# A searched instruction order, searched again: one more edge on a PSUM bank, other order, buffers and spins

## The chip, the cores and the metric

The kernel runs on one core of one Trainium2 chip. The metric is the device time of one execution in microseconds (us). Engines are called by the profile's letters: PE is TensorE (PEld its weight loads), DVE is VectorE, ACT is ScalarE, POOL is GpSimd, SP is SyncE, which here only starts DMA transfers.

## The reference

Two blocks follow each other. The first is a linear attention with squared sketches, over 4 batches, 4 heads, 1088 positions and head size 32 (sketch size r = 8):

```python
def phi(x):
    a = np.einsum('rd,bhsd->bhsr', S1, x)
    b = np.einsum('rd,bhsd->bhsr', S2, x)
    return np.einsum('bhsi,bhsj->bhsij', a, b).reshape(*x.shape[:-1], r * r)
q_p, k_p = (phi(q), phi(k))
kv = np.einsum('bhsf,bhsd->bhfd', k_p, v)
z = np.sum(k_p, axis=2)
num = np.einsum('bhsf,bhfd->bhsd', q_p, kv)
den = np.einsum('bhsf,bhf->bhs', q_p, z)[..., None] + 1e-06
return (num / den).astype(np.float32)
```

The second takes that output with the heads side by side (4 x 1088 x 128) as x and mixes positions by two 1088 x 1088 weights:

```python
theta = x @ w_theta
cos_t, sin_t = (np.cos(theta), np.sin(theta))
zr = x * cos_t
zi = x * sin_t
yr = np.einsum('ts,bsd->btd', w_tok_r, zr)
yi = np.einsum('ts,bsd->btd', w_tok_i, zi)
y = yr + yi
u = x + y
return (u + np.maximum(u @ w_ch, 0.0)).astype(np.float32)
```

All is in 32-bit floats; weights may come as 64-bit words, which ACT and DVE turn into floats row by row.

## The kernel before, in words

The kernel does not issue its work as its loops run. Each step is recorded by `op(engine, duration, function, writes, reads)` (class `Layout`), which notes for it the steps that it must follow, by the buffers that it writes and reads or by keys that name a part of a buffer. 1015 steps are recorded and numbered so. Then three tables, written out by hand into the file from a search that was made beforehand, decide all the rest. `ORDER` lists the steps' numbers in the order in which they are issued, for all engines in one list; each engine runs its own steps in that order, and a step that waits holds up all behind it on its engine. `PLACES` gives each buffer its home, one of the numbered slots of its class (22 of `big`, 8 PSUM banks `ps`, and so on); two buffers in one home follow each other, and the second's first step waits for the first's last one. `SPINS` lists steps ahead of which TensorE does some matmuls on zeros (line 377), "step:count". `issue` walks through `ORDER` and calls each step's function. Waits between engines come from a layer below, which looks at each tile that an instruction touches. For a PSUM bank it takes the whole bank: an instruction that reads a bank waits for the last matmul issued ahead of it into that bank, and a matmul issued behind it into that bank waits for the read.

The work, in the program's order (batches are 0 to 3):

- Loads by SP, in SP's order: keys `k_l`, queries `q_l`, values `v_l` of each batch (576 KB each), keys of batches 2 and 3 once more (`r`), the two small weights, and 17 rows of the token weights (1088 KB each, into five `zs` homes). For each row ACT makes two passes and DVE two sums (row 0 to row 16).
- `key_sums`, `kfeatures`, `chain`, `chain_out`: keys are split into a rounded part and a rest, their Gram matrix is summed on TensorE (64 or 128 columns at a time), features are made and multiplied with the values (`kv`); a chain of some 25 short steps that go to and fro between DVE, ACT and TensorE (`chain`) gives the normaliser. Chains are run for batch 0, batch 1 and batches 2 and 3 together.
- `query_scale`, `query_slices`, `levels`, the den steps: queries are scaled and turned, multiplied with the normaliser's slices, and DVE works out the denominator in nine wide steps.
- `outputs_x`: for each of three groups `num`, an outer product on DVE, is turned by TensorE (line 1042; batches 2 and 3 turn it by DMA) and multiplied with the key-value matrix; `theta`, cosine, sine give z.
- Batches 0 and 1: `mix_row` multiplies all 17 rows with z on TensorE, 384, 384 and 320 columns wide.
- Batches 2 and 3 are a pair: `balance` sets their scale, and `winograd` mixes them in Strassen's way with seven products for eight: `zsub` and `asum` make differences of z and of the weight rows on DVE, `product` does the matmuls of one product into two PSUM banks (`PARTS`: columns 0 to 288 and 288 to 544), and `add` (line 1260) adds a bank, or a piece of one, into the output on DVE. Only the last product, number 4 for batch 2, is cut once more, at column 416 (`LAST`), so that its second bank holds two pieces, 288 to 416 and 416 to 544. Each piece is added by itself and is then turned, multiplied with the channel weight and stored (`done`, `finish_turned`), the end of the program.

What the change touches: `ORDER` (line 27), `PLACES`, `SPINS` and `add`. In `add`, the list of reads names the piece's keys:

```python
op("V", dve(w) + 0.05, lambda: tt(V, u(), u(), ps()[:, o:o + w], ALU.add), k_, parts_of(ps, o, w))
```

The prediction's steps are found so: first keys at `load(0, "k")`; the first outer product at `vop(CH * R * R, lambda f=outer: f(V, 0, 1), ...)` in `outputs_x`, its transpose at line 1042; the levels of batch 1 at `lev` in `levels`; joins at `join` (a DMA from POOL that adds into its target); the stop in the tail at `add` of product 4.

Of the kernel before, what the change touches and what calls it, by code (L numbers as in the profile page):

```python
# [17 lines left out]
ALU = mybir.AluOpType  # L18
# [8 lines left out]
TINY = 2.0**-60  # L27
UP = 256.0
ORDER = (
# [37 lines left out]
)  # L67
PLACES = (
# [9 lines left out]
)  # L78
SPINS = (
    "76:2 15:2 84:2 89:6 135:1 189:1 166:3 439:2 521:1 1005:1 "  # L80
)
WARM = 0
SPLIT = ()
# [5 lines left out]
PARTS = ((0, 288), (288, 544))  # L89
# [130 lines left out]
def dve(n):  # L220
    return (n + 145) / 960.0
# [15 lines left out]
def kernel(  # L237
# [52 lines left out]
    op, buf = L.op, L.buf  # L290
# [4 lines left out]
    V, A, G, T, SY = nc.vector, nc.scalar, nc.gpsimd, nc.tensor, nc.sync  # L295

    def fixed(shape, dt, name):
        b = Buf(None, shape, dt, name)
        n = math.prod(shape) * WORD[dt]
        b.ap = view(const.tile([P, (n + 3) // 4], F32, tag=name, name=name), shape, dt)  # L300
        return b

    def tt(eng, o, a, b, f):
        eng.tensor_tensor(out=o, in0=a, in1=b, op=f)  # L304
# [5 lines left out]
    def stt(o, a, s, b, op0, op1, eng=None):  # L310
        (eng or V).scalar_tensor_tensor(out=o, in0=a, scalar=s, in1=b, op0=op0, op1=op1)  # L311
# [117 lines left out]
    def powers(mfn, m, n, name):  # L429
# [7 lines left out]
        def inv():  # L437
# [16 lines left out]
                                    op=ALU.max, apply_absolute_value=True), [m2], [(sp, 0)])  # L454
# [435 lines left out]
    even = fixed((6,), F32, "even")  # L890
# [5 lines left out]
    def cells(x, t0, t1):  # L896
        return [(x, j) for j, (e0, e1) in enumerate(zip(EDGES, EDGES[1:])) if t0 < e1 and t1 > e0]
# [305 lines left out]
    def winograd():  # L1203
# [30 lines left out]
        def parts_of(ps, o, w):  # L1234
            e = sorted({0, GW} | {x - c0 for c0, c1 in PARTS for x in LAST if c0 < x < c1})
            return [(ps, a) for a, b in zip(e, e[1:]) if o < b and o + w > a]
# [22 lines left out]

        def add(b, h, j, c0, c1, ps):  # L1260
            o, w = c0 - PARTS[j][0], c1 - c0
            c0, c1 = c0 + h * HT, c1 + h * HT
            u = lambda: xT[b]()[:, c0:c1]
            k_ = cells(xT[b], c0, c1)
            if b == p:
                op("V", dve(w) + 0.05, lambda: tt(V, u(), u(), ps()[:, o:o + w], ALU.add), k_, parts_of(ps, o, w))
            else:
                op("V", dve(w) + 0.06, lambda: stt(u(), ps()[:, o:o + w], even()[:, 5:6], u(), ALU.mult, ALU.add), k_,
                   parts_of(ps, o, w) + [even])

        def done(b, h, last=()):
            for m, (_, c0, c1) in enumerate(pieces(last)):
# [20 lines left out]
        for j in range(len(PARTS)):  # L1293
            at("accl", q, "_", j)
            ps = buf("ps", (GW,), F32, "pl")
# [99 lines left out]
```

## Time and profile before

| what | us |
| --- | --- |
| median of three runs | 221.3 (220.59, 221.3, 222.36) |
| the profiled execution, its own time | 219.88 |
| its span, first to last instruction | 218.1 |
| PE busy | 209.8 |
| DVE busy | 179.1 |
| ACT busy | 112.0 |
| POOL busy | 22.8 |

The mean granted clock of TensorE is 0.995 of full speed. The span is 1.8 us shorter than the execution's own time. In the profile a matmul of 32-bit floats shows as two records, a transpose or one of 16-bit numbers as one. A matmul's record begins when it begins, but its length is longer than the step to the next one, since matmuls are pipelined: a busy PE need not be at its peak, and steps are read from the starts. A wait is shown in brackets behind an instruction, with what released it.

### The profile page before, as it was taken

Reading aid. Unit: us, or ns where it says so; the run is one execution under the profiler, and the core shown is the slowest. Engines: PE = TensorE matmul, PEld = TensorE weight load, DVE = VectorE, ACT = ScalarE, POOL = GpSimd, SP = SyncE. Lnnn points to the kernel's source line nnn. Section 1 sums busy time; section 2 is a strip of 40 time slices with the busy share of each in tenths; the row PEclk is TensorE's granted clock in tenths of the full one; section 3 lists DMA queues with packets and bytes.
Section 4 is the critical chain, followed back from the end, with each engine's and each line's share of the span. In section 5 each row is a group of like instructions: output and inputs, shape, how many; then the busy total and the mean of one; then the engine's idle time right before and its main releaser. Section 6 shows DMA issues by size and latency. Waiting matters only on the chain.

```text
span 218.1 us, 5091 instructions
## 1 busy us (share of the span) xinstructions
PE 209.8 (96%) x2012; PEld 155.3 (71%) x2012; DVE 179.1 (82%) x404; ACT 112.0 (51%) x216; POOL 22.8 (10%) x44
## 2 busy tenths in 40 slices
PE   6999899999999999999999999999999999999993
PEld 3788687677767676665866665678767888888882
DVE  4789999999999999999399709985829999996531
ACT  3898998999988998953640032433168100000000
POOL 1552000005500000010302001000400000000000
PEclk9999999999999999999999999999999999999998
DMA  5999399895999709955423998668980000405163
GB/s 162 426 416 410 110 419 410 297 370 179 257 307 405 302 13 388 378 146 161 101 33 50 188 179 199 118 107 172 236 155 0 0 0 3 72 2 86 20 92 75
DMA packets 48108, 40.59 MB, mean 186 GB/s; under 512 B 40789, under 2 KB 42453, under 8 KB 45909
## 3 DMA queue, kind: packets, MB, share of 16 engines
q1 hardware_dynamic: 42820, 35.18, 51.3%
q0 software_dynamic: 1728, 4.65, 9.8%
q10 hardware_dynamic: 3536, 0.43, 1.3%
q8 instruction: 16, 0.26, 0.5%
q14 instruction: 8, 0.06, 0.1%
HBM read 30.43 MB, written 5.18 MB: 163 GB/s over the span
## 4 chain that ended last, share of the span: by engine, by line
PE 85%; DVE 10%; DMA 2%; issue 1%; ACT 0%; SPq 0%; ACTq 0%; DVEq 0%
PE ps L339 77%; PE ps L1042 2%; DVE big L304 2%; DMA big<-k_l 2%; DVE g L304 2%; PE ps L1076 2%; PE ps L945 1%; DVE lv L304 1%; PE ps L377 1%; PE ps L721 1%; DVE sm L311 1%; DVE big L308 1%; DVE hf L308 1%; DVE sm L304 1%; SPq L392 0%
## 5 line engine op out<-in xcount | busy, mean ns | idle before, releaser
L339 PE MATMUL ps<-big,zs 128*128 128x384 f32 (+4 forms) x398 | 111.1, 425 | 0.4 <-DVE big L304 0.4
L339 PEld LDWEIGHTS ps<-big,zs 128*128 128x128 f32 x398 | 71.2, 190 | 29.9 <-issue 2.6
L1179 ACT COPY g<-ps 128x128 f32<-128x128 f32 (+1 forms) x3 | 0.9, 301 | 43.8 <-DMA out<-g 39.5
L584 ACT ACTIVATE big<-zs 128x1088 int32<-128x1088 uint32 (+1 forms) x18 | 21.1, 1187 | 3.4 <-DVE g L304 2.2
L304 DVE CUSTOM_DVE_ANT_0 big<-big,big 128x2176 uint16<-128x2176 uint16 x17 | 21.7, 1284 | 0.1
L582 ACT ACTIVATE big<-zs 128x1088 f32<-128x1088 f32 x17 | 20.7, 1223 | 0.6 <-DVE big L304 0.6
L339 PE MATMUL ps<-big,big 128*64 128x64 f32 (+2 forms) x208 | 20.9, 275 | 0.0
L339 PEld LDWEIGHTS ps<-big,big 128*64 128x64 f32 (+1 forms) x208 | 16.7, 154 | 2.8 <-issue 0.4
L304 DVE TENSOR_TENSOR big<-big,big 128x544 f32<-128x544 f32 x24 | 16.6, 709 | 1.2 <-PE ps L339 1.1
L980 ACT COPY lv<-ps 128x480 f32<-128x480 f32 x12 | 6.6, 565 | 16.1 <-PE ps L339 16.1
L318 POOL DMA_DIRECT2D big<-hf x6 | 5.7, 994 | 80.1 <-issue 37.3
L308 DVE TENSOR_SCALAR big<-big 128x1088 int32<-128x1088 int32 x17 | 12.2, 730 | 0.0
L339 PEld LDWEIGHTS ps<-w,big 128*128 128x128 f32 x80 | 10.8, 192 | 1.2
L339 PE MATMUL ps<-w,big 128*128 128x128 f32 x80 | 11.5, 277 | 0.0
L304 DVE TENSOR_TENSOR g<-lv 128x768 f32<-128x768 f32 x12 | 11.3, 947 | 0.1
L1089 ACT ACTIVATE g<-ps 128x384 f32<-128x384 f32 x12 | 5.9, 494 | 9.6 <-PE ps L339 4.4
L311 DVE SCALAR_TENSOR_TENSOR g<-g,ps 128x384 f32<-128x384 f32 x12 | 6.6, 547 | 4.7 <-ACT g L1089 4.7
L339 PE MATMUL ps<-g,sm 128*64 128x384 f32 x48 | 10.0, 502 | 0.0
L377 PE MATMUL ps<-idle 128*128 128x384 bf16 x32 | 8.7, 387 | 1.3 <-POOL idle L379 1.3
L318 POOL DMA_DIRECT2D g<-big x6 | 5.2, 923 | 44.8 <-ACT g L1157 26.8
L339 PEld LDWEIGHTS <-hf 128*64 128x64 f16 (+1 forms) x288 | 7.4, 110 | 3.2 <-issue 1.9
L304 DVE TENSOR_TENSOR zs<-ps,g 128x768 f32<-128x768 f32 (+2 forms) x15 | 9.4, 627 | 0.0
(188 smaller groups left out, 338.5 us busy)
## 6 DMA issues: line engine op xcount, KB each, us to landing
zs<-w_tok SPq DMA_DIRECT2D x17, 1088.0 KB, 7.6
big<-k_l SPq DMA_DIRECT2D x6, 576.0 KB, 8.9
big<-hf POOLq DMA_DIRECT2D x6, 576.0 KB, 5.4
big<-q_l SPq DMA_DIRECT2D x4, 576.0 KB, 7.0
big<-v_l SPq DMA_DIRECT2D x4, 576.0 KB, 5.4
fq<-g SPq DMA_DIRECT2D x24, 96.0 KB, 2.9
g<-fq SPq DMA_DIRECT2D x6, 384.0 KB, 3.8
g<-big POOLq DMA_DIRECT2D x4, 192.0 KB, 4.9
```

Source lines behind the costliest of these rows:

```text
L304: eng.tensor_tensor(out=o, in0=a, in1=b, op=f)
L308: (eng or V).tensor_scalar(out=o, in0=a, scalar1=s1, scalar2=s2, op0=op0, **kw)
L311: (eng or V).scalar_tensor_tensor(out=o, in0=a, scalar=s, in1=b, op0=op0, op1=op1)
L318: op("G", 0.9, lambda: G.dma_start(dst(), src(), accum_op=ALU.add), w, r, fly=fly)
L339: T.matmul(o, lhs, rhs, start=start, stop=stop, skip_group_check=True)
L377: T.matmul(nowhere() if home is None else view(home, (GW,), F32), idle()[:, 0:P], idle(), start=True, stop=True, skip_group_check=True)
L582: op("A", 0.22 + n * 0.0009, lambda: A.activation(dfn(), words_of(raw(), n)[1].bitcast(F32), AF.Prelu, scale=2.0**-112, alpha=-(2.0**32)), ...
L584: op("A", 0.22 + n * 0.0009, lambda: A.activation(stp(), words_of(raw(), n)[0].bitcast(U32), AF.Copy, scale=2.0**-29), [stp], [raw])
L980: op("A", act(480), lambda g=g, lp=lp: A.copy(lv().rearrange("p l (c n) -> p l c n", n=HR)[:, :, g * GC:(g + 1) * GC], lp().rearrange("p c ...
L1042: T.transpose(tr()[:, i * P:(i + 1) * P], qp()[:, i * H + 2 * n:i * H + 2 * n + 2].rearrange("p h i j -> p (h i j)"), ident())
L1076: T.transpose(x()[:, i * P:(i + 1) * P], xs()[:, off + i * P:off + (i + 1) * P], ident())
L1089: op("A", act(GW), lambda cs=cs, th=th: A.activation(cs()[:, 0], th(), AF.Copy, bias=ROUND), [(cs, 0)], [th])
```

## The change

One line is added in `add`, and its result is used in both branches: a sum whose columns end where its bank's columns end reads the whole bank, not only its piece. For the banks with one piece nothing becomes different by that. For product 4's second bank it means that the sum of columns 416 to 544 must stand behind the last matmul of columns 288 to 416 in any order that the search may give.

```diff
         def add(b, h, j, c0, c1, ps):
             o, w = c0 - PARTS[j][0], c1 - c0
+            r = [ps] if c1 == PARTS[j][1] else parts_of(ps, o, w)
             c0, c1 = c0 + h * HT, c1 + h * HT
             u = lambda: xT[b]()[:, c0:c1]
             k_ = cells(xT[b], c0, c1)
             if b == p:
-                op("V", dve(w) + 0.05, lambda: tt(V, u(), u(), ps()[:, o:o + w], ALU.add), k_, parts_of(ps, o, w))
+                op("V", dve(w) + 0.05, lambda: tt(V, u(), u(), ps()[:, o:o + w], ALU.add), k_, r)
             else:
                 op("V", dve(w) + 0.06, lambda: stt(u(), ps()[:, o:o + w], even()[:, 5:6], u(), ALU.mult, ALU.add), k_,
-                   parts_of(ps, o, w) + [even])
+                   r + [even])
```

`ORDER` and `PLACES` are replaced as a whole. The steps and what they compute stay the same, 1015 in number; on TensorE 59 of 360 steps keep their place in its sequence, on DVE 65 of 344, on ACT 38 of 207, on POOL 14 of 38, on SP 30 of 66, and most of the others move by a few places. The end of both lists, where 970 to 998 are product 4 (980 to 988 the piece 288:416, 990 to 998 the piece 416:544), 989 and 999 the sums of those pieces, and 1005 to 1014 the last outputs:

```diff
-    "961 976 960 977 978 963 917 964 979 995 965 983 1000 984 1001 996 997 985 1002 998 986 1004 1003 999 987 988 "
-    "1010 1011 989 1012 966 1005 1013 1006 1007 1014 1008 1009 "
+    "985 964 979 986 923 992 916 963 1000 917 918 993 1001 987 994 988 1002 995 989 996 1004 1003 997 965 998 1005 "
+    "1006 999 1007 966 1010 1008 1011 1012 1009 1013 1014 "
```

The spins become 26 from 21 (and ten at the start in both):

```diff
-    "76:2 15:2 84:2 89:6 135:1 189:1 166:3 439:2 521:1 1005:1 "
+    "76:2 15:2 89:2 72:3 111:2 315:3 426:3 166:4 172:2 174:2 1010:1 "
```

Here 76, 89, 72 are steps of batch 0's keys, 111 of its chain, 315 a transpose of batch 1's queries, 426 the levels of batch 0, 166, 172 and 174 the chain of batch 1, 439 the first transpose of `num`, 521 the levels of batch 1. SP's order of loads begins k0, q0, w2, k1, q1, row 1, k2, v0, row 2, k3, row 0, v1, row 5, row 3 before, and k0, k1, q0, q1, row 1, w2, v0, k2, k3, row 2, row 3, row 5, row 0, r3, v1 after.

88 rows, old and new, of tables (ORDER, PLACES) are left out of this document.

## Prediction

> **What bounds the kernel now.** I read the page's busy line and slices first, then the busy time of four stretches, the timelines around their borders, and last TensorE's waits.
>
> ```profile
> PE 209.8 (96%) x2012; PEld 155.3 (71%) x2012; DVE 179.1 (82%) x404; ACT 112.0 (51%) x216; POOL 22.8 (10%) x44
> PE   6999899999999999999999999999999999999993
> DVE  4789999999999999999399709985829999996531
> PEclk9999999999999999999999999999999999999998
> ```
> TensorE looks full everywhere and its clock is granted throughout, so the question is what fills it.
>
> ```profile
> 0.00:40.60 40.60, 36.37 (x710) 28.85 (x710) 34.44 (x120) 33.37 (x72) 8.62 (x29) 1.00 0.83 328
> 40.60:46.76 6.16, 6.16 (x61) 4.16 (x61) 6.09 (x22) 5.94 (x13) 0.00 (x0) 1.00 0.98 373
> 46.76:212.10 165.34, 165.34 (x1232) 120.94 (x1232) 137.40 (x260) 72.12 (x131) 14.19 (x15) 1.00 0.58 149
> 212.10:218.10 6.00, 1.93 (x14) 1.33 (x12) 1.15 (x4) 0.53 (x2) 0.00 (x0) 0.84 0.33 68
> ```
> Columns: stretch, length, then busy PE, PEld, DVE, ACT, POOL, clock, DMA share, GB/s. From 46.76 to 212.10 TensorE never rests. In the first stretch 8.02 of its 36.37 us are spins (30 matmuls of line 377 that do nothing); there VectorE sets the pace.
>
> ```profile
> 39.63 0.34 PE L377 MATMUL ps<-idle 128*128 128x384 bf16 x1
> 39.97 0.48 PE L377 MATMUL ps<-idle 128*128 128x384 bf16 x2
> 40.60 0.87 PE L1042 MATMUL ps<-ident,g 128*128 128x128 f32 x6
> 46.49 0.34 PE L377 MATMUL ps<-idle 128*128 128x384 bf16 x1
> 46.76 0.57 PE L339 MATMUL ps<-mv,hf 128*64 128x96 f16 x18
> ```
> ```profile
> 39.59 0.95 DVE L304 TENSOR_TENSOR g<-lv 128x768 f32<-128x768 f32 x1
> 40.72 0.95 DVE L304 TENSOR_TENSOR g<-lv 128x768 f32<-128x768 f32 x1
> 41.67 0.95 DVE L304 TENSOR_TENSOR g<-lv 128x768 f32<-128x768 f32 x1
> ```
> At 40.60 TensorE, spinning, gets the first outer product of queries (`num`, VectorE 39.59 to 40.54). From there, but for one spin, it has work without a gap. So time = start of that transpose + TensorE's stream behind it + tail.
>
> ```profile
> 212.43 0.29 DVE L304 TENSOR_TENSOR big<-big,ps 128x128 f32<-128x128 f32 x1 [0.37 <-PE ps L339]
> 212.77 0.71 PE L339 MATMUL ps<-big,zs 128*128 128x128 f32 x4 [0.38 <-DVE big L304]
> 213.52 0.29 DVE L304 TENSOR_TENSOR big<-big,ps 128x128 f32<-128x128 f32 x1 [0.81 <-PE ps L339]
> ```
> ```profile
> PE ps L339 <- DVE big L304: 0.4, 1, 0.4
> ```
> In the tail TensorE stops once: product 4 has two open pieces (columns 288:416 and 416:544) in one bank; the second piece's sum on VectorE stands between the first piece's matmuls, which wait for it.
>
> **The change, part by part.** "Ahead of" means: the durations of an engine's instructions that stand before a point in an order, each counted until the next one starts, added up from the timeline of this one execution (span 218.10, time 219.88).
>
> *1. The new edge.* It adds one constraint: the sum of 416:544 stands behind the last matmul of 288:416. The new order obeys by swapping the pieces. But now the sum of 288:416 stands between matmuls of 416:544: in the built program that sum waits for the matmul just before it, and the next matmul waits for the sum, exactly as before. So the stop is not removed but handed to the other piece. Before: one matmul, stop, two matmuls, then the last sum; after: one, stop, three, last sum. Behind the waiting sum VectorE queues only the last two output sums, behind the stopped matmul stand the last transposes, all of which need the sums anyway. Between, VectorE now does the 256-wide output of batch 3 (0.42 at 210.21), hidden by three matmuls of 2 x 0.11 = 0.66; if they were quicker, the last sum would be late by the difference. Value 0; bounds -0.5 (stop gone: 0.38 idle plus a re-start of 0.1) and +0.4 (that output uncovered).
> The row is the 0.38. The Trainium skill, "PSUM — Partial Sum Buffer", section "PSUM bank collisions raise a hardware error", says that engines have to be kept apart by semaphore per bank and quadrant, not per address. By that rule two sums over one bank always cost one stop, and this edit gains nothing; by its title it would gain 0.5. The trace agrees with the rule.
>
> *2. The start, to the first `num` transpose.* Ahead of the first outer product VectorE has 33.43 us of work in the old order, 33.63 in the new. Old idle: 39.59 - 33.43 = 6.16, of which 4.57 lie before its first keys (load of k0) and 1.6 are short waits. Following the new order by hand over the same rows, I find these waits elsewhere (the key product now waits for the squares of k1, a 1.17 row of ACT; the scale of q0 is put ahead of the chain) but of like sum: at the chain's nu (16.90 ahead in both) I get 22.9 against 22.95. So +0.2. Bounds: all 1.6 gone, -1.4; a second such wait, +0.7. There are five spins more (26 for 21, 0.16 to 0.32 each by their starts). They stand ahead of matmuls that wait for VectorE or ACT: the four new ones in batch 1's chain have as cover the 0.22 idle before its 128x64 product at 38.37 and the three old spins from 39.63, which go. If that cover were gone, two spins would be late by 0.3, inside the bound.
> The loads change order (k1 before q0; row 3 early and row 0 late; v1, r3 behind them in SP's queue). Row 8 is issued near 45 and used near 52: 7 us against a median landing of 7.6. It is covered, since its reader runs on ACT (5.94 of 6.16 busy, but 72.12 of 165.34 later) and its row is needed after 88. On POOL the join of k3's rest is issued 1.3 us later in VectorE's order; the four joins of 576 KB land over 9 us from 53, so this one near 57.6, 1.2 before its matmuls at 58.83. The join ahead of it now starts 3 us sooner, so it does not queue: 0.
>
> *3. TensorE's stream behind it.* From 40.60 to the last matmul before the stop (212.00) are 171.41 us. Each kind of matmul at its usual step (128x384: two of 0.325; 128x288: two of 0.243; and so on) makes 166.25 with the spin at 46.49; the rest, 5.16, lies at its 37 changes of array tile (128x128 to 128x64 and such): 0.14 each. The new order puts batch 1's three key-value sums behind this point and one feature group before it, and drops the spin: 166.50, with 34 changes: 166.50 + 34 x 0.139 = 171.24. So -0.2; bounds -0.6 and 0.
>
> *4. New waits in the stream.* Where a producer and its matmul move relative to each other, I compared what is ahead of each. Second and third outer product stand 1.9 and 2.7 us later on VectorE (34.53 to 36.47; 35.47 to 38.16), their transposes also: 0.35 to 0.6 us of room is left. The rows' last sums before mix keep 0.7 or more. The products of batches 2 and 3 (165 to 200) are tight: VectorE is 9.8 and 10.0 of 10 busy at 170 to 190, the old order leaves 0.17 to 0.30 us at eight places, the new one, counted from `balance` (137.42 ahead in both), 0.02 to 0.22 at seven. A semaphore's passage is some 0.06 in these rows, so a few of these may bind: I take +0.2; bounds 0 and +2 (three such places each behind one more 0.64 sum of weights).
>
> Sum: +0.0 + 0.2 - 0.2 + 0.2 = +0.2 on 219.88, so 220.1 for an execution like the profiled one. That one was 1.4 below the median of the runs (221.3), so 221.5.
>
> **Rivals.**
> *Slower by the Strassen part* (0.19): VectorE's sums of weight rows come late for TensorE. For it: 0.02 us of room. Against it: VectorE enters this part waiting for TensorE both times (3.5 us idle before 160.86), and the old order with 0.2 ran through. It decides where VectorE is more than 0.2 late after `balance`; three sums of 0.64 late is +1.9 on top: 223.4.
> *Faster at the start* (0.09): the 1.6 us of VectorE's waits before the first `num` disappear and TensorE's stream starts at 39.2: -1.6 against my +0.2, so 219.7, and with the tail's stop gone 219.2. Against: the key product at the start still waits for ACT.
> *The first edit does what its name says* (0.05): 0.5 less, 221.0.
> *Exposed fetches of TensorE's instructions* (0.07): q8 moved 16 packets in 0.5% of 16 x 218.1, 1.1 us each; TensorE's gaps all have another releaser. If denser bursts outran two fetches, +1.5: 223.0. The Trainium skill, "Runtime: NRT & Kernel Launch", section "Instruction fetch mechanics", has the sequencer fetch the next 256 instructions while it runs the present ones, mostly hidden. By it this is 0, as the trace bears out so far.
>
> **How the numbers follow.** My forecast, with all within 1 us of it, has 0.60: 221.5, 220.5 to 222.5. Of the 0.26 on the slow side about 0.18 end over 223.5 and 0.12 over 223.9; of the 0.14 on the fast side 0.08 end below 219.1. The range 219.1 to 223.9 leaves out about 0.2 of the cases; it takes in the start's -1.4, the slow part's +1.9 and the runs' own scatter (220.59 to 222.36). Over 1% (2.2 us, about what a measurement of this kernel can tell from no change): faster 0.08, same 0.74, slower 0.18.
>
> **What would show it.** Step 1: a TensorE wait of 0.3 to 0.4 on a 128x128 sum some 6 us from the end. Step 2: the first L1042 transpose at 40.6 to 40.9. Step 3: from it to the stop 171.0 to 171.5, no spin at levels of batch 1. Step 4: TensorE's waits on `big` L304 between 165 and 200 below 0.5 in sum. I am wrong if the first transpose is off by over 1 us, or if TensorE's waits behind it exceed 1 us.

## The result, and the profile after

The changed kernel takes 222.24 us (median of 20 runs, 221.46 to 223.53), the kernel before 220.36 in as many runs beside it (219.63 to 222.65): ratio 1.008, 95% interval 1.0059 to 1.0101. It is slower by 1.9 us, less than 1%. The forecast's 221.5 lies nearer to 222.24 than its reasons deserve, and that is luck: it was +0.2 on a base of 221.3, the median of three runs, and twenty give the base as 220.36, so that a base too high by 0.9 hid more than half of a change too low by 1.7. The change to be explained is +1.9, not +0.2. Ratios, here and below, are taken over the fast runs alone and are not the quotients of the medians (a run of e_sj of 738.77 us and a few of the kernel before are slow and not in them).

The profiled execution after took 221.75 with a span of 220.0 (before: 219.88 and 218.1). The page's busy line, then the busy time of four stretches with the columns that the prediction gives:

```profile
PE 210.9 (96%) x2017; PEld 155.8 (71%) x2017; DVE 178.4 (81%) x404; ACT 111.9 (51%) x216; POOL 23.7 (11%) x44
```
```profile
0.00:40.14 40.14, 36.95 (x656) 28.64 (x656) 34.26 (x121) 32.93 (x73) 9.42 (x29) 1.00 0.84 325
40.14:46.88 6.74, 6.74 (x120) 5.16 (x122) 6.63 (x22) 6.62 (x15) 0.00 (x0) 1.00 0.72 264
46.88:213.38 166.50, 165.30 (x1232) 120.52 (x1228) 136.12 (x258) 71.91 (x129) 14.32 (x15) 1.00 0.59 152
213.38:220.00 6.62, 1.87 (x13) 1.46 (x13) 1.41 (x5) 0.43 (x2) 0.00 (x0) 0.98 0.34 69
```
In the third stretch the kernel before was busy for the whole of it. Here 166.50 hold 165.30: TensorE rests for 1.2 us. The last stretch is 0.6 longer than before (6.62 for 6.00). The start is earlier, 40.14 for 40.60; TensorE's timeline there:

```profile
40.14 0.87 PE L1042 MATMUL ps<-ident,g 128*128 128x128 f32 x6
```
The holes behind it are found in TensorE's timeline by the brackets:

```profile
58.66 1.27 PE L339 MATMUL ps<-big,big 128*64 128x64 f32 x36 [0.28 <-DMA big<-hf]
...
78.54 0.98 PE L339 MATMUL ps<-g,big 128*32 128x64 f32 x54 [0.26 <-issue]
...
160.30 0.83 PE L339 MATMUL ps<-w,big 128*128 128x128 f32 x6
161.75 0.78 PE L339 MATMUL ps<-g,w 128*128 128x320 f32 x2 [0.62 <-DMA g<-big]
```
At 58.66 batch 3's rest (step 253) waits for the join that POOL issued at 53.03. At 78.54 batch 2's key-value sum (194) waits for its features, which VectorE ends at 78.44. At 161.75 the channel product of batch 1's third group (646) waits for a join too. Between 165 and 200, where the prediction put its new waits, there is none:

```profile
165.00:200.00 35.00, 35.00 (x161) 28.65 (x160) 33.76 (x68) 4.71 (x10) 0.00 (x0) 1.00 0.13 21
```
And the tail, all engines:

```profile
211.57 3.90 ACTq L1193 DMA_DIRECT2D out<-g  x4
...
213.76 0.94 PE L339 MATMUL ps<-big,zs 128*128 128x128 f32 x6 [0.38 <-DVE big L304]
...
214.73 0.29 DVE L304 TENSOR_TENSOR big<-big,ps 128x128 f32<-128x128 f32 x1 [0.69 <-PE ps L339]
...
215.24 0.39 PE L339 MATMUL ps<-w,big 128*128 128x128 f32 x2
215.65 0.43 ACT L1179 COPY g<-ps 128x128 f32<-128x128 f32 x2 [5.72 <-DMA out<-g]
```
The stop of 0.38 is there as foreseen. New is ACT: the transposes that its two last copies wait for end at 214.80 and 215.40, and the copies start at 215.65 and 215.81, behind four stores that ACT takes 3.90 us to issue.

With each kind of matmul at the step that it usually takes in the trace before, and 0.139 for a change of array tile, the two spans compare so (a gap is named by the start of the matmul ahead of it):

| part (us) | before | after | difference |
| --- | --- | --- | --- |
| start of the first `num` transpose | 40.60 | 40.14 | -0.46 |
| usual steps to the last matmul, with spins | 167.54 | 168.03 | +0.49 |
| changes of array tile (37, 34) | 5.14 | 4.73 | -0.42 |
| more than that at 58.1, ahead of step 253 | 0 | 0.45 | +0.45 |
| at 78.0, ahead of 194 | 0 | 0.31 | +0.31 |
| at 160.7, ahead of 646 | 0.10 | 0.78 | +0.68 |
| at 42.1, a change from 128x64 to 128x32 with no releaser shown | 0 | 0.16 | +0.16 |
| all other gaps, the stop of 0.54 in the tail among them | 0.65 | 0.64 | 0.0 |
| start of the last matmul (214.03, 215.24) to the end | 4.08 | 4.73 | +0.65 |
| span | 218.11 | 219.97 | +1.86 |

### The profile page after: what moved, and what is told of

Its sections match the earlier page's. It is cut to its first block, busy times and chain, and to the rows that moved or that the text cites. A ratio compares the mean times of both kernels' runs of the same rounds, so it can differ in the third digit from the quotient of the medians.

```text
span 220.0 us, 5099 instructions
## 1 busy us (share of the span) xinstructions
PE 210.9 (96%) x2017; PEld 155.8 (71%) x2017; DVE 178.4 (81%) x404; ACT 111.9 (51%) x216; POOL 23.7 (11%) x44
## 4 chain that ended last, share of the span: by engine, by line
PE 65%; DVE 15%; DMA 11%; ACT 3%; issue 3%; SPq 2%; DVEq 0%
PE ps L339 59%; DVE big L304 3%; DMA big<-hf 2%; DMA g<-fx 2%; DMA g<-big 2%; DMA big<-k_l 2%; DVE g L304 2%; DVE hf L308 2%; SPq L332 2%; PE ps L1042 1%; DVE lv L304 1%; PE ps L945 1%; PE ps L1076 1%; ACT big L584 1%; PE ps L721 1%
## 5 line engine op out<-in xcount | busy, mean ns | idle before, releaser
L339 PE MATMUL ps<-big,zs 128*128 128x384 f32 (+4 forms) x398 | 109.9, 424 | 0.4 <-DVE big L304 0.4
L339 PEld LDWEIGHTS ps<-big,zs 128*128 128x128 f32 x398 | 71.6, 190 | 31.3 <-issue 3.0
L339 PE MATMUL ps<-big,big 128*64 128x64 f32 (+2 forms) x208 | 20.7, 276 | 0.3 <-DMA big<-hf 0.3
L339 PEld LDWEIGHTS ps<-big,big 128*64 128x64 f32 (+1 forms) x208 | 16.5, 154 | 3.1 <-issue 0.5
L339 PEld LDWEIGHTS ps<-w,big 128*128 128x128 f32 x80 | 10.9, 192 | 2.0 <-issue 0.6
L339 PE MATMUL ps<-w,big 128*128 128x128 f32 x80 | 11.5, 277 | 0.0
L377 PE MATMUL ps<-idle 128*128 128x384 bf16 x37 | 9.7, 380 | 1.6 <-POOL idle L379 1.3
L339 PE MATMUL ps<-g,sm 128*64 128x384 f32 x48 | 10.4, 505 | 0.0
L308 DVE TENSOR_SCALAR big<-lv 128x576 f32<-128x576 f32 x4 | 1.8, 455 | 9.7 <-ACT lv L980 9.7
L339 PEld LDWEIGHTS <-hf 128*64 128x64 f16 (+1 forms) x288 | 7.6, 110 | 2.8 <-issue 1.9
```

The costliest lines, as they stand in the source:

```text
L308: (eng or V).tensor_scalar(out=o, in0=a, scalar1=s1, scalar2=s2, op0=op0, **kw)
L339: T.matmul(o, lhs, rhs, start=start, stop=stop, skip_group_check=True)
L377: T.matmul(nowhere() if home is None else view(home, (GW,), F32), idle()[:, 0:P], idle(), start=True, stop=True, skip_group_check=True)
```

## The experiments

Theory: the new order let in four waits that have nothing to do with VectorE's load, each from one step that stands in another place of one engine's queue: POOL's two joins, batch 2's features, and ACT's stores. Rivals: the new order is slower by its whole, so that a wait taken away comes back elsewhere; or the edit of `add` itself costs. Most kernels move single steps, named by their numbers in `ORDER`, and the other engines keep their sequences. The kernel before ran beside them with medians of 220.37 (e_swap, e_join, e_tail, e_jt), 220.19 (e_sj, e_k3, e_lane, e_all) and 219.95 (the other four).

| run | median us | ratio to before | 95% |
| --- | --- | --- | --- |
| e_swap | 220.11 | 0.9999 | 0.9969 to 1.0029 |
| e_nostop | 220.11 | 0.9996 | 0.9972 to 1.0019 |
| e_join | 222.01 | 1.0092 | 1.0062 to 1.0123 |
| e_tail | 221.72 | 1.0081 | 1.0054 to 1.0108 |
| e_jt | 222.39 | 1.0089 | 1.0056 to 1.0123 |
| e_sj | 221.82 | 1.0054 | 1.0031 to 1.0078 |
| e_k3 | 221.83 | 1.0070 | 1.0041 to 1.0100 |
| e_lane | 221.15 | 1.0043 | 1.0017 to 1.0068 |
| e_all | 221.09 | 1.0022 | 0.9998 to 1.0045 |
| e_best | 221.59 | 1.0070 | 1.0049 to 1.0092 |
| e_best_ns | 221.28 | 1.0064 | 1.0043 to 1.0086 |
| e_start | 222.03 | 1.0091 | 1.0076 to 1.0107 |

### e_swap: the first edit alone

The kernel before with steps 980 to 989 and 990 to 999, and 1005 to 1009 and 1010 to 1014, exchanged.

```diff
-    ... 986 1004 1003 999 987 988 1010 1011 989 1012 966 1005 ...
+    ... 996 1004 1003 989 997 998 1005 1006 999 1007 966 1010 ...
```


> The first edit alone: the kernel before, with the two pieces of product 4's second bank exchanged (all steps of 288:416 in the places of those of 416:544 in the order and in the homes, and the other way round), so that the sum of 416:544 stands behind the last matmul of 288:416 as the new edge wants it. All else is as before. The prediction's step 1: the stop is handed to the other piece, TensorE waits 0.38 some 6 us from the end as before, value 0, ratio 0.999 to 1.001. Rival (the edit does what its name says): the wait is gone and the ratio is 0.998, 0.5 us less.

Measured 0.9999. TensorE's timeline (this file is two lines shorter, L337 is L339):

```profile
212.80 0.71 PE L337 MATMUL ps<-big,zs 128*128 128x128 f32 x4 [0.38 <-DVE big L302]
```
The stop is the same 0.38 with the other piece in front. The Trainium skill, "PSUM — Partial Sum Buffer", section "PSUM bank collisions raise a hardware error", keeps engines apart per bank and quadrant and not per address; by that rule one stop has to stay, and it did. The last rival needs no run: what `add` lists as read is noted by `op`, but `issue` walks through `ORDER` alone, so that the changed line by itself alters no instruction.

### e_nostop: no sum between the matmuls

The kernel before with 999 behind 988, so that both sums follow all matmuls.

```diff
-    ... 1004 1003 999 987 988 1010 ...
+    ... 1004 1003 987 988 999 1010 ...
```


> The kernel before with one step moved: the sum of columns 416:544 (step 999) stands behind the last matmul of 288:416 too (988), so that both pieces' matmuls run without a sum between them and both sums follow. Theory A (the one stop of 0.38 in the tail is the price of reading a bank between matmuls into it, and goes only when no sum stands between them): TensorE's wait on `big` in the middle of product 4's last matmuls is gone, a shorter one stands ahead of the first turned output, the last matmul starts 0.2 to 0.35 earlier, ratio 0.998 to 0.9995. Theory B (the sum in between hid the first output's work, so the same 0.4 is waited behind the last matmul): last matmul as before, ratio 1.000.

Measured 0.9996. The stop has moved to the first turned output, with the same length:

```profile
213.33 0.33 PE L1171 MATMUL ps<-ident,big 128*128 128x128 f32 x1 [0.38 <-DVE big L304]
```
From the first `num` transpose to the last matmul it takes 173.31 for 173.43. So even what the name of the edit promises is worth 0.1 here: TensorE has nothing else left to do, and waits once whichever way. The prediction's rival had priced it at 0.5. The edit is neither gain nor loss.

### e_join: ACT's copy 644 ahead of 621

The join that step 646 waits for (645) is issued by POOL when ACT has copied its target (644). ACT's and POOL's timelines after:

```profile
155.04 0.48 ACT L1157 COPY g<-ps 128x384 f32<-128x384 f32 x1 [7.13 <-PE ps L339]
155.42 0.53 ACT L1092 ACTIVATE g<-g 128x384 f32<-128x384 f32 x1
155.84 0.42 ACT L1157 COPY g<-ps 128x320 f32<-128x320 f32 x1
```
```profile
156.55 1.75 POOL L318 DMA_DIRECT2D g<-big  x2 [19.52 <-DMA g<-fx]
```
The copy of 320 columns is 644. Its matmuls end at 153.93, but ACT sits for 7.13 us in front of 621, whose matmuls end at 155.00. The bracket of POOL names a transfer, yet the join starts 0.29 after the copy's end (156.26), as it does before (154.19, 154.49). In the kernel before 644 stands ahead of 621.

```diff
-    ... 620 784 621 803 710 735 644 645 785 ...
+    ... 620 784 644 621 803 710 735 645 785 ...
```


> The changed kernel with one step moved: ACT's copy of the last channel product's input of batch 1 (step 644) is issued ahead of the copy of the middle one (621) instead of two steps behind it. On the other engines nothing moves. Theory A (the wait of 0.62 at 161.75 comes from ACT's order: 644's matmuls end at 153.93, but the copy stands behind 621, whose matmuls end at 155.00): the copy runs at 154.0 instead of 155.84, POOL's join is issued near 154.3 instead of 156.55, lands near 159.5, TensorE's wait for the join is gone and the rest of the stream is 0.6 to 0.7 earlier: span 219.3 for 220.0, ratio to the kernel before 1.0055 for 1.0085. Theory B (the join is late because the transfer queues are, ACT's order is not the cause): landing and wait stay, 1.0085. Theory C (VectorE's small room in the Strassen part): the wait at 161.75 goes but TensorE then waits for sums of weights between 165 and 200, and under 0.3 is left of the gain.

Measured 1.0092, no gain. The copy ran at 154.16, the join was issued at 154.88 and step 646 no longer waited, as theory A has it; but a step 2.5 us ahead of it now did (one line fewer in this file, L338 is L339):

```profile
159.23 0.87 PE L338 MATMUL ps<-g,sm 128*64 128x384 f32 x4 [0.48 <-DMA g<-fq]
...
161.72 0.70 PE L338 MATMUL ps<-g,w 128*128 128x320 f32 x2
```
That is the product of batch 3's second group (741), which waits for SP's read-back of its turned queries (740). Theory A was incomplete, and theory C wrong about the place. In e_jt, below, the same wait is 1.83.

### e_sj: SP's read-back 740 ahead of 707 as well

SP's timeline after, and its read-backs in the kernel before:

```profile
150.69 2.98 SPq L332 DMA_DIRECT2D fq<-g  x4
153.77 0.94 SPq L336 DMA_DIRECT2D g<-fx  x1
154.88 1.60 SPq L336 DMA_DIRECT2D g<-fq  x2
```
```profile
152.85 2.15 SPq L336 DMA_DIRECT2D g<-fq  x3
```
SP has no gap from 143.71 on; 740 stands behind 707 (153.77) and goes at 154.88, in the kernel before at 153.66. TensorE starts the product at 158.19 in the kernel before and at 158.48 after.

```diff
-    ... 811 801 707 783 517 812 831 802 740 838 ...
+    ... 811 801 740 707 783 517 812 831 802 838 ...
```


> The changed kernel with two steps moved: on SP the read-back of batch 3's second turned group (step 740) is issued ahead of that of theta's third group of batch 2 (707) instead of behind it; on ACT copy 644 stands ahead of 621, as in the run e_join. Theory A (what was won in e_join and e_jt by the earlier join was taken again by SP's queue: 740 is issued at 154.9 to 155.7 there, 153.66 in the kernel before, and TensorE waited 0.48 and 1.83 for its landing): 740 is issued near 153.8, lands near 157.8, and neither the wait for `fq` (line 339, about 158 to 159) nor the one for the join (161.75) is left: excess of TensorE's stream 0.6 to 0.8 less than in the changed kernel, ratio 1.004 to 1.006 for 1.0085. Theory B (the transfers themselves are slower here, three at once): the read-back still takes 4 to 5.4 us from issue to landing with the join beside it, and a wait of 0.5 or more stays at 158 to 162.

Measured 1.0054, 0.6 us less than the changed kernel by the ratios (0.3 by the medians), with intervals that overlap; so the trace decides. Neither 741 nor 646 waits (excess under 0.15 at both); 740 is issued at 154.44, and TensorE stands 0.7 later here than in the profile after (644's matmuls end at 154.62 for 153.93, since it lost 1.02 to the join of k3's rest), so that is 153.75 against 154.88. So this place is settled: two late issues, ACT's and SP's, behind one another, and curing only one moves the wait to the other. (In e_tail, where the joins stand as in the changed kernel, product 741 waits 0.27 too: its read-back has no room in the new order.)

### e_tail, e_jt and e_lane: ACT's stores

```diff
-    ... 989 996 1004 1003 997 ... 1011 1012 1009 1013 1014 
+    ... 989 996 1003 997 ... 1011 1012 1004 1009 1013 1014 
```


> The changed kernel with one step moved: the two stores that ACT issues for an output of batch 2 (step 1004) stand behind ACT's two last copies (1007, 1012) instead of ahead of them. Theory A (ACT's queue: its store of 1004 stands until 215.15 for an earlier transfer, and the copies behind it start at 215.65 though their transposes were done at 214.80 and 215.40): the copies start at 214.85 and 215.45, VectorE's last sum near 215.75 instead of 216.16, the last stores are issued 0.4 to 0.7 earlier, span 219.3 to 219.7 for 220.0, ratio 1.0055 to 1.007 for 1.0085. Theory B (the copies wait for the earlier store from the same home, as the bracket of the profile names a store): the copies stay at 215.65 and the time at 1.0085. Theory C: the moved stores are the last to land, so that the span does not shrink though the copies are early.

Measured 1.0081. Theory C held: the copies came right behind their transposes (214.06, and 214.66 with the last matmul at 214.46), but the moved stores landed last, and from the last matmul to the end it still took 4.59.

> Both moves at once (644 ahead of 621, 1004 behind 1012) on the changed kernel. Theory A: the two gains add up, 1.0 to 1.4 us in all, span 218.6 to 219.0, ratio 1.002 to 1.004. Theory C (VectorE binds in the Strassen part): only the tail's gain is seen, 1.006 to 1.007.

Measured 1.0089; both moves together gained nothing, for the reasons that e_join and e_tail show one by one. TensorE's timeline of its profiled execution, the slowest of its seven (223.43), has the read-back at its worst:

```profile
161.26 0.87 PE L338 MATMUL ps<-g,sm 128*64 128x384 f32 x4 [1.83 <-DMA g<-fq]
```
Why does ACT take 3.90 for four stores that took 0.4 to 0.5 each before? The layer below deals eight semaphores in turn to the transfers of SP and ACT (0 to 7 here), and a transfer whose semaphore is in use waits for the one that has it. In the trace after, ACT's last four stores (two of step 918, two of 1004) stand so:

| ACT's store | issued | semaphore | who has it, until when |
| --- | --- | --- | --- |
| 918, first | 211.57 | 4 | free |
| 918, second | 213.25 | 5 | SP's store issued at 211.57, until 213.23 |
| 1004, first | 213.75 | 6 | SP's store issued at 211.93, until 213.67 |
| 1004, second | 215.16 | 7 | SP's store issued at 213.30, until 215.13 |

In the kernel before these four stores have 1, 3, 3 and 5, whose holders had landed. The Trainium skill, "DMA: Bandwidth & Descriptors", section "Anatomy of one DMA — SWDGE (gpsimd) path", has any semaphore wait of a transfer happen on the engine that issues it; it says so of GpSimd's path, and the trace agrees for ACT, which neither issues nor computes for 1.1 and 1.0 us. e_lane takes the collision away without moving any work of the tail: the stores of 923 go 6 us earlier, and all later transfers get other semaphores.

```diff
-    ... 922 972 958 ... 979 986 923 992 ...
+    ... 922 923 972 958 ... 979 986 992 ...
```


> The changed kernel with one step moved: ACT's two stores for an output of batch 3 (step 923, its sum done at 203.46) stand right behind SP's two for the same output instead of three steps of ACT later. The program gives each transfer one of eight semaphores in turn, and one whose semaphore is in use waits for the transfer that has it. By the move ACT's later stores get other semaphores: the second of 1004 that of a store 211.6 instead of one issued at the same time by SP. Theory A (this wait holds ACT until 215.15 and with it the two last copies): the stores are issued without a stop, the copies start at 214.85 and 215.45 for 215.65 and 215.81, and the span ends 4.0 to 4.2 after the start of the last matmul, as in the kernel before, for 4.76: ratio 1.005 to 1.006. Theory B (the time of the last transfers sets the end whatever ACT does): the distance from the last matmul to the end stays near 4.6.

Measured 1.0043, 0.8 less than the changed kernel, though the intervals still touch (1.0017 to 1.0068, 1.0059 to 1.0101). The tail of e_lane, all engines:

```profile
214.84 0.27 ACT L1179 COPY g<-ps 128x128 f32<-128x128 f32 x1 [4.78 <-PE ps L1171]
...
215.24 0.39 PE L339 MATMUL ps<-w,big 128*128 128x128 f32 x2
215.44 0.27 ACT L1179 COPY g<-ps 128x128 f32<-128x128 f32 x1 [0.33 <-PE ps L1171]
215.74 0.29 DVE L311 SCALAR_TENSOR_TENSOR g<-ps,g 128x128 f32<-128x128 f32 x1 [0.31 <-ACT g L1179]
```
The last matmul starts at 215.24 as in the profile after, and the span ends at 219.28 for 219.97: 4.04 behind it, about the distance before (4.08). ACT issues its last four stores without a stop.

### e_k3: the join of k3's rest, issued earlier

```diff
-    ... 525 484 355 469 373 526 249 379 ...
+    ... 525 484 249 355 469 373 526 379 ...
```


> The changed kernel with one step moved: VectorE makes the rest of batch 3's keys (step 249, 0.45 us) ahead of two wide steps (355 of 0.71 and 526 of 0.75) instead of behind them. Theory A (the join of k3's rest is issued too late by VectorE's order; it landed at 58.52 in the profile after, for matmuls that could start at 58.37, and 0.4 to 1.0 us late in the runs e_join and e_jt): POOL issues it near 51.7 instead of 53.03, it lands near 57.2, TensorE's wait for it at 58 to 59 is gone, 0.3 to 0.6 is won: ratio 1.006 to 1.007 for 1.0085. Theory B (the four transfers of 576 KB around 48 to 60 share the engines, so an earlier issue lands no earlier): the wait stays. Theory C: the two wide steps, now 0.45 later, make something else late, and nothing is won.

Measured 1.0070; 0.2 less than the changed kernel, inside the intervals. POOL's timeline after, and that of e_k3:

```profile
53.03 0.86 POOL L318 DMA_DIRECT2D big<-hf  x1 [3.86 <-DVE hf L308]
53.63 1.85 POOL L308 TENSOR_SCALAR qs<-qs,ec 128x1 f32<-128x1 f32 x1
55.42 1.79 POOL L318 DMA_DIRECT2D big<-hf  x2
```
```profile
51.58 0.86 POOL L318 DMA_DIRECT2D big<-hf  x1 [2.56 <-DVE hf L308]
52.17 1.25 POOL L308 TENSOR_SCALAR qs<-qs,ec 128x1 f32<-128x1 f32 x1
52.73 2.45 POOL L318 DMA_DIRECT2D big<-hf  x2
```
The join goes 1.45 earlier, but so do the two of 576 KB behind it, 2.7. Issue and landing of this join, and of the one ahead of it on POOL, in four traces:

| kernel | the join ahead | the join of k3's rest |
| --- | --- | --- |
| before | 51.08, landed 55.47 | 52.31, landed 57.94 |
| after | 48.10, landed 56.44 | 53.03, landed 58.52 |
| e_k3 | 47.95, landed 56.21 | 51.58, landed 58.30 |
| e_all | 48.68, landed 57.72 | 52.30, landed 59.79 |

So theory B holds for most of it: 1.2 of the 1.45 went into a longer transfer, 6.7 from issue to landing for 5.5. (The Trainium skill, "DMA: Bandwidth & Descriptors", section "Issuing engines are not separate DMA queues": transfers of all issuers run on the same 16 engines and interleave. The trace agrees; their busy share from 52 to 56 was 1.06 here and 0.98 after.)

The table says why an earlier issue could win so little. In all ten kernels with the whole new order the join lands 2.07 to 2.10 us behind the one ahead of it, whether it was issued 3.6 us behind that one or 4.9. And the one ahead, which the new order issues 3 us sooner than the kernel before, lands 1.0 later: it takes 8.3 us after for 4.4. From 50 to 52, when the one ahead is on its way after and just issued before, the DMA engines are full after and nearly idle before:

```profile
50.00:52.00 2.00, 2.00 (x19) 1.60 (x15) 2.00 (x5) 2.00 (x5) 0.92 (x1) 1.00 0.14 51
```
```profile
50.00:52.00 2.00, 2.00 (x13) 1.35 (x10) 2.00 (x4) 2.00 (x5) 0.00 (x0) 1.00 1.02 373
```
The first line is before, the second after (DMA share 0.14 and 1.02). From 48 to 52 the queue of SP's loads (q1) moved 1.56 MB after, 0.79 before. That these loads delay the join ahead is read from the traces and not shown: no run moves them.

### e_all, e_best, e_best_ns: together

e_all has the moves of e_sj, e_k3 and e_lane, and

```diff
-    ... 194 320 200 270 391 568 206 606 207 ...
+    ... 606 194 320 200 270 391 568 206 207 ...
```


> The moves of e_sj, e_k3 and e_lane together, and on TensorE one matmul group of batch 1's rows (step 606) ahead of batch 2's key-value sums (194), which in the changed kernel wait 0.33 for VectorE. Theory A (the loss of the changed kernel is the sum of these four places, each a wait that the new order lets in): 1.8 to 2.2 less than the changed kernel, 220.0 to 220.4, ratio 0.998 to 1.001. Theory B (the new order is slower by its whole, waits appear elsewhere when these go): more than 0.8 of it stays, ratio over 1.004.

Measured 1.0022: 1.3 us of the 1.9 are gone by the ratios (0.0058 of 220.2), 1.0 by the medians, and the interval just holds 1. What is left in its profile is one wait, for the join of k3's rest: excess 1.12 at 58.7, TensorE's only gap over 0.4 ahead of the tail. With a start at 40.74 (+0.15) and the gap of 0.16 at the start's end it accounts for its span of 219.5, 1.4 over that of the kernel before. Theory A, but for the place that e_k3 could not cure. So e_best left 249 where it was and gave TensorE the next row meanwhile:

```diff
-    ... 187 474 253 378 533 221 363 487 534 ...
+    ... 187 474 378 533 221 363 487 253 534 ...
```


> The moves of e_all but for the join: VectorE's step 249 stays where the changed kernel has it, and on TensorE the matmuls of batch 3's rest (253), which wait for the join, stand behind batch 0's next row (487) instead of ahead of it, two steps later. Theory A (in e_all the join of k3's rest, issued 1 us earlier, landed later, 7.5 us after its issue for 5.5, since two more joins of 576 KB that stand behind it on POOL were let go 2.7 us earlier too; TensorE is to be given other work instead): the wait of 0.45 to 1.1 at 58 becomes 0.3 or less (row 487 waits for VectorE's z until 58.8), the other waits are as in e_all, 219.8 to 220.4, ratio 0.998 to 1.000. Theory B (what comes behind batch 3's rest is then late, by up to 1.5): ratio over 1.002.

Measured 1.0070, worse than e_all. Theory B. Its timelines of TensorE and ACT:

```profile
59.23 0.38 PE L339 MATMUL ps<-sm,ones 128*128 128x1 f32 x2 [0.47 <-DVE zs L304]
...
64.29 0.34 PE L339 MATMUL ps<-ident,g 64*64 64x64 f32 x4 [0.73 <-ACT g L680]
```
```profile
62.80 1.21 ACT L582 ACTIVATE big<-zs 128x1088 f32<-128x1088 f32 x1 [1.57 <-PE ps L339]
63.91 0.20 ACT L679 COPY g<-ps 128x64 f32<-128x64 f32 x1
```
The wait for the join is gone, and two others came: row 487 stands 0.47 for its z, and ACT stands 1.57 in front of a pass of row 6 (step 368). That pass writes the home of k3, which step 253 still reads; behind it stands the copy 254 that TensorE's next product needs. The table of homes made a step of ACT wait for one that I had moved on TensorE. (A third wait of this profile, 0.41 at 161.17 for a z, is not in that of e_best_ns.)

> e_best with the sum of 288:416 (989) behind the last matmul of 416:544 too, as e_nostop does it in the kernel before. Theory A: 0.2 to 0.35 less than e_best, ratio 0.997 to 0.999, the fastest of all. Theory B of e_nostop: as e_best.

Measured 1.0064: not to be told from e_best, as e_nostop would have it. Of the versions with the new order none beats the kernel before; e_all comes nearest.

### e_start: the start alone

> The start alone: the changed kernel's order and spins up to the first transpose of `num` (step 439), then the order of the kernel before for all that is left. The homes are those of the kernel whose order gives the step, 46 of 422 dealt anew where two would overlap. Theory A (the start's gain is mostly work put off: TensorE's first transpose comes 0.46 earlier, but with 0.89 less work done ahead of it, three key-value sums of batch 1, so that at the rows of mix both kernels stand alike): first transpose near 40.1 to 40.6, ratio 0.999 to 1.002. Theory B (the start is a gain of its own that the later waits ate): ratio 0.997 to 0.999. The newly dealt homes may add waits of their own; the trace shows them.

Measured 1.0091. The first transpose came at 40.09, and then TensorE waited for ACT three times:

```profile
43.21 0.55 PE L1042 MATMUL ps<-ident,g 128*128 128x128 f32 x3 [0.45 <-ACT g L1046]
...
46.31 0.94 PE L339 MATMUL ps<-w,big 128*128 128x128 f32 x6 [0.62 <-ACT g L1046]
...
52.95 0.94 PE L339 MATMUL ps<-w,big 128*128 128x128 f32 x6 [0.35 <-ACT lv L980]
```
Theory B (a gain of its own) gets no support: with the start of the one and the rest of the other, the 0.5 won is lost within 13 us to these waits, 1.4 in sum. Theory A is not shown by it either, since the seam itself makes ACT late, and 46 homes are not those of either kernel.

## Why the prediction was right or wrong

By its own mark (TensorE's waits behind the first transpose exceed 1 us) it was wrong about the mechanism, though 222.24 lies within its range and the change within 1%: the brackets give 0.28, 0.26, 0.62 and the stop's 0.38, 1.5 in sum, where the kernel before has the stop alone. That the time itself came within 0.8 of the forecast is due to the base that was too high.

1. *New edge, 0.* Right: the stop was handed to the other piece, 0.38 in both, and alone it is worth nothing (e_swap); its upper bound, the 256-wide output uncovered, did not bind: the last sum starts 0.04 after its matmul. What failed is the sentence on who is queued behind: it looked at VectorE's and TensorE's queues and not at ACT's stores. That is +0.65, shown by e_lane, and in no term of the sum. Nor is the third matmul behind the stop, which the text names: +0.22.
2. *The start, +0.2.* Too high, inside its bounds: -0.46 in this profile. VectorE's work ahead of the first outer product is 33.24 us (the step had 33.63, and 33.43 in the kernel before), and its idle time there 5.89 for 6.16. The ten kernels with this order as a whole lie between 40.02 and 40.74, on the mean 40.27, against 40.60, 40.60 and 40.68 with the old one. The spins cost nothing. The step that failed is the join of k3's rest, costed at 0 with 1.2 us to spare because "the join ahead of it now starts 3 us sooner, so it does not queue". That join started 3 us sooner and landed 1.0 later (56.44 for 55.47), and the one behind it landed 2.08 after that: at 58.52, not 57.6. Step 253 could start near 58.2, not 58.83; so +0.45 here, and up to 1.2 in other runs, where the join ahead landed at 57.1 to 57.7 (e_sj, e_jt, e_all).
3. *TensorE's stream, -0.2.* Right: usual steps and changes together are +0.07 to the last matmul, and -0.15 without the third matmul behind the stop.
4. *New waits, +0.2 between 165 and 200.* Wrong in place and size: nothing there, +0.68 at 161 and +0.31 at 78. The step counted the work ahead of each producer on VectorE and ACT. It did not see that a copy can stand behind one whose matmuls end later (644 behind 621), nor SP's queue, full from 143.7 to 155, in front of two transfers that TensorE needs.

Of the rivals, "slower by the Strassen part" named the side and not the place: VectorE had 0.02 us of room there and it sufficed. Every gap that is 0.2 or more above the usual step and tile change has its releaser or a producer that ends with it, so exposed fetches of instructions have nothing to explain; q8 moved the same 16 packets.

What stays open: the gap of 0.16 at 42.1, which recurs in all ten kernels with the whole new order and not in e_start; what delays the join ahead of k3's rest; and whether the start can be had without its waits.

## What to carry to other kernels

When an order is changed, go through the transfers as through the matmuls: for each one that the bound engine needs, who issues it, what stands ahead of it in that queue (a copy that waits for a later product, a store that waits for a semaphore), and how long it took at worst, not once. A transfer issued earlier lets go all that is queued behind it, and may land no sooner when another one of its queue is still on the way. A wait cured at one step shows the next one behind it, so cure them together before judging one.

## What the runs showed of the hardware that was not expected

- One join of 576 KB took 5.0 to 6.5 us from issue to landing in kernels that issue it at the same step (e_tail 5.0, e_lane 5.2, after 5.5, e_join 5.6, e_sj 6.2, e_jt and e_best_ns 6.3, e_best 6.5), and 6.7 and 7.5 (e_k3, e_all) where it and two more were let go earlier. In all ten it landed 2.07 to 2.10 us behind the join ahead of it on POOL, which took 7.9 to 9.3 us; with the old order it was 2.4 to 2.5, and the one ahead took 4.4 to 4.5.
- A read-back of 384 KB took 3.2 us from issue to landing after, 3.9 in e_tail, 4.0 in e_join and 5.4 in e_jt; the last two had a join of 160 KB issued 0.2 ahead of them alike, so the join alone does not explain the 5.4.
